# Exponentials of 1024 columns in place of 768 in a fused attention and expert kernel

## The chip, the core and the metric

The kernel runs on one core of a Trainium2 chip. The metric is the time on the device in microseconds (us), the median of several executions. The profile is one execution of the same program, and its span is a little shorter than the measured time. Engines: PE is the matrix engine, PEld its weight loads, DVE the vector engine, ACT the activation engine, POOL the general engine, and SP the engine whose instruction queue issues nearly all DMAs here.

## The reference

```python
# q, k, v: (4 batches, 8 heads, 768 positions, 64); proj: (64, 6)
q_bucket = sum over 6 bits of (q @ proj > 0) * 2**bit       # the same for k
mask     = q_bucket[..., :, None] == k_bucket[..., None, :]
scores   = where(mask, q @ k.T / 8, -1e9)
attn     = softmax(scores) @ v                               # (4, 8, 768, 64)
x        = attn, heads side by side                          # (3072, 512)
h        = x @ w_in                                          # (3072, 2048)
g        = h + sin(alpha * h)**2 / (alpha + 1e-9)
out      = g @ w_out                                         # (3072, 512)
```

## The kernel before

The program is a list of 16 pairs of heads, `pairs[i]`, four to a batch. A pair has 12 steps: two heads, six blocks of 128 keys each. A step multiplies one key block with all 768 queries (scores, transposed: keys in the partitions), takes the exponential on ACT, and some steps later "weighs" the values with it: six matmuls, one for each block of 128 queries. The hash mask is folded into the contraction as 12 extra rows, so a score matmul has 76 rows.

```python
HALF = S // 2                       # 384
banks = psum.tile([128, 8, 512], FP32, name="banks")
turns = deque(range(3))             # banks 0..5 are three slots of two banks

def slot(hold=False):
    n = turns.popleft()
    if not hold:
        turns.append(n)             # it comes round again at once; its readers are waited for
    return banks[:, 2 * n:2 * n + 2, :], n
def give_back(n):
    turns.append(n)

def attend(i, at_step, lag=3):
    ...
    for n in range(2 * SB):         # 12 steps
        hh, kb = divmod(n, SB)
        sc, _ = slot()
        for half in range(2):       # 384 queries in each bank
            nc.tensor.matmul(out=sc[:, half, 0:HALF], lhsT=ka[...key block kb...],
                             rhs=qa[0:KA, hh, half * HALF:(half + 1) * HALF], ...)
        e = e_pool.tile([128, S], BF16, name="e")
        nc.scalar.activation(out=e..., in_=sc[:, :, 0:HALF], func=AF.Exp, scale=SCALE)
        behind.append((i, hh, kb, e, accs[hh], xn))
        at_step(n)                  # the work between two steps, see below
        while len(behind) > lag + (i > NPAIR and behind[0][2] == 0):
            weigh(behind.pop(0))    # after key block 5: finish_head
```

`at_step(n)` puts parts of the preparation of later pairs, and a share of the contraction of the batch before (`g @ w_out`), between two steps. Pairs 1 to 5 are prepared on PE (hash matmuls, picking of bits, four times six transposes), and hold one of the three slots from their first transposes to the end of them; later pairs are prepared by DMA.

```python
def prepare_on_pe(i):
    ...                                   # hash and picking in bank 6 (i > 1)
    ps, held = slot(hold=True)            # at step 3 of pair i - 1
    for h in range(2):
        for t in (0, 1):
            ... six transposes into ps[0:KA, t, ...], copied out by DVE
            yield                         # steps 3, 4, 6, 7
    ...
    give_back(held)                       # at step 9

def prepare_by_dma(i):
    ...
    for a, nat in zip(aug, nats):         # step 6 of pair i - 2
        nc.sync.dma_start_transpose(out=a..., in_=nat...)               # qa<-qn, ka<-kn
    ps, held = slot(hold=True)            # step 10: hash matmuls, bits
    for a in range(4):
        nc.sync.dma_start(out=rows[...], in_=bits[a::4]...)             # rows<-bits
    ... give_back(held)                   # step 11
    ... copies of qa and ka               # step 1 of pair i - 1
    for t in range(2):                    # step 3 of pair i - 1
        for n in range(2):
            nc.sync.dma_start(out=aug[t][...], in_=rows...)             # qa<-rows, ka<-rows

def finish_head(i, hh, acc, xn):
    ...                                   # DVE: add the base, divide
    if hh == 1:
        nc.sync.dma_start_transpose(out=xt[b][:, hp, :]..., in_=xn...)  # xt<-xn
```

The expansion of a batch (`x @ w_in`, sine, square) reads `xt`; it comes after the first pair of the next batch, the last one at the end. So the program alternates: attention of five pairs, expansion, attention of four pairs, expansion, and so on.

The softmax here doesn't subtract the row's maximum and nothing guards it: scores larger than these inputs give would overflow.

Of the kernel before, what the change touches and what calls it, by code (L numbers as in the profile page):

```python
# [10 lines left out]
BF16 = mybir.dt.bfloat16  # L11
AF = mybir.ActivationFunctionType
# [11 lines left out]
def kernel(  # L24
# [11 lines left out]
    nc = tc.nc  # L36

    B, H, S, D = q.shape
# [3 lines left out]
    SB = S // 128  # L42
    NPAIR = H // 2
    NF = DFF // 128
    NP = DMODEL // 128
    HALF = S // 2
    KA = D + 2 * NB
    ON_PE = 6
    SCALE = 1.0 / (D ** 0.5)
# [5 lines left out]
    v32_pool = ctx.enter_context(tc.tile_pool(name="v32", bufs=3))  # L55
    v_pool = ctx.enter_context(tc.tile_pool(name="vp", bufs=4))
    w_pool = ctx.enter_context(tc.tile_pool(name="w32", bufs=3))
    e_pool = ctx.enter_context(tc.tile_pool(name="ep", bufs=6))
    x_pool = ctx.enter_context(tc.tile_pool(name="xp", bufs=3))
    xt_pool = ctx.enter_context(tc.tile_pool(name="xt", bufs=2))  # L60
    moe_pool = ctx.enter_context(tc.tile_pool(name="moe", bufs=3))
    g_pool = ctx.enter_context(tc.tile_pool(name="gp", bufs=1))
    o_pool = ctx.enter_context(tc.tile_pool(name="op", bufs=4))
    dram = ctx.enter_context(tc.tile_pool(name="scratch", bufs=4, space=bass.MemoryType.DRAM))
    psum = ctx.enter_context(tc.tile_pool(name="ps", bufs=1, space=bass.MemoryType.PSUM))

# [7 lines left out]
# [6 lines that stand above are left out]
# [102 lines left out]
    def turn_blocks(name, src):  # L182
        t = hash_pool.tile([128, 2, SB, 2, 32], FP32, name=f"{name}t")
        nc.vector.transpose(  # L184
            out=t.rearrange("p h s b c -> p (h s b c)"),
            in_=src.rearrange("p h s d -> p (h s d)"),
        )
        return t
# [32 lines left out]
    def prepare_on_pe(i):  # L221
# [3 lines left out]
        turned = [turn_blocks("q", q2)]  # L225
        nat = hash_pool.tile([128, SB, 4, KA], BF16, name="nat")
        for t, src in enumerate((q2, k2)):
# [22 lines left out]
        for s in range(SB):  # L250
# [5 lines left out]
        nc.vector.tensor_copy(  # L256
            out=nat[:, :, :, D:KA], in_=picked.rearrange("p s (j m) -> p s j m", j=4))
        yield
# [4 lines left out]
        for h in range(2):  # L263
            if (i, h) == (0, 1):
                ps = banks[:, 6:8, :]
            for t in ((1, 0) if i == 0 else (0, 1)):
                out = ps[0:KA, t, 0:HALF].bitcast(BF16)
                for s in range(SB):
                    nc.tensor.transpose(out[:, s * 128:(s + 1) * 128], nat[:, s, 2 * t + h], ident)  # L269
                if (i, h, t) == (0, 0, 1):  # L270
                    nc.scalar.copy(out=aug[t][0:KA, h, :], in_=out)
                else:
                    nc.vector.tensor_copy(out=aug[t][0:KA, h, :], in_=out)  # L273
                yield
# [64 lines left out]
    def finish_head(i, hh, acc, xn):  # L339
        b, hp = pairs[i]  # L340
        rden = hash_pool.tile([128, SB], FP32, name="rden")
        cols = acc[:, 0:SB * (D + 1)].rearrange("p (s e) -> p s e", e=D + 1)
        if len(operands[i]) > 4:
            total = x_pool.tile([128, SB, D + 1], FP32, name="total")
            nc.vector.tensor_tensor(  # L345
                out=total, in0=cols,
                in1=operands[i][4][:, hh].unsqueeze(1).to_broadcast([128, SB, D + 1]), op=ALU.add,
            )
            cols = total
        nc.vector.reciprocal(out=rden, in_=cols[:, :, D])  # L350
        nc.vector.tensor_tensor(  # L351
            out=xn[:, :, hh, :], in0=cols[:, :, 0:D],
            in1=rden.unsqueeze(2).to_broadcast([128, SB, D]), op=ALU.mult,
        )
        if hh == 1:
            nc.sync.dma_start_transpose(
                out=xt[b][:, hp, :].rearrange("p (s c) -> p s c", s=SB),
                in_=xn.rearrange("p s h d -> p (s h d)"),
            )

    behind = []

    def weigh(step):
        i, hh, kb, e, acc, xn = step
        vaug, vsum = operands[i][2:4]
        regions = acc[:, 0:SB * (D + 1)]

        apart = len(operands[i]) > 4
        if kb == 0 and not apart:
            nc.tensor.matmul(  # L370
                out=regions.rearrange("p (s e) -> p s e", e=D + 1),
                lhsT=empty,
                rhs=vsum[:, hh, :].unsqueeze(1).to_broadcast([128, SB, D + 1]),
                start=True, stop=False,
            )
        for qb in range(SB):
            nc.tensor.matmul(  # L377
                out=regions[:, qb * (D + 1):(qb + 1) * (D + 1)],
                lhsT=e[:, qb * 128:(qb + 1) * 128],
                rhs=vaug[:, hh, kb, :],  # L380
                start=(apart and kb == 0 and qb == 0), stop=(kb == SB - 1 and qb == SB - 1),
            )
        if kb == SB - 1:
            finish_head(i, hh, acc, xn)

    def attend(i, at_step, lag=3):
        b, hp = pairs[i]
        if b not in xt:
            xt[b] = xt_pool.tile([128, NPAIR, S], BF16, name="xt")
        qa, ka = operands[i][0:2]  # L390
        accs = [banks[:, 6, :], banks[:, 7 if i <= NPAIR else 6, :]]
        xn = x_pool.tile([128, SB, 2, D], BF16, name="xn")
        for n in range(2 * SB):
            hh, kb = divmod(n, SB)
            sc, _ = slot()
            for half in range(2):
                nc.tensor.matmul(  # L397
                    out=sc[:, half, 0:HALF],
                    lhsT=ka[0:KA, hh, kb * 128:(kb + 1) * 128],
                    rhs=qa[0:KA, hh, half * HALF:(half + 1) * HALF],  # L400
                    start=True, stop=True,
                )
            e = e_pool.tile([128, S], BF16, name="e")
            nc.scalar.activation(  # L404
                out=e.rearrange("p (h c) -> p h c", h=2), in_=sc[:, :, 0:HALF],
                func=AF.Exp, scale=SCALE,
            )
            behind.append((i, hh, kb, e, accs[hh], xn))
            at_step(n)

            while len(behind) > lag + (i > NPAIR and behind[0][2] == 0):
                weigh(behind.pop(0))
# [3 lines left out]
    def expand(b, at_chunk):  # L416
        g = g_pool.tile([128, NF, S], BF16, name="g")
        def close(F, s2, h):
# [3 lines left out]
                scalar=inv_alpha[:, F:F + 1],  # L422
                in1=h[:, :, 0:HALF],
                op0=ALU.mult, op1=ALU.add,
            )

        for F in range(NF):
            at_chunk(F, g)
            h = banks[:, 6:8, :] if F in (3, 7, 11) else slot()[0]
            for half in range(2):  # L430
                for p in range(NP):
                    nc.tensor.matmul(  # L432
                        out=h[:, half, 0:HALF],
                        lhsT=w_in_bf[:, p, F * 128:(F + 1) * 128],
                        rhs=xt[b][:, p, half * HALF:(half + 1) * HALF],
                        start=(p == 0), stop=(p == NP - 1),
                    )
            while behind:
                weigh(behind.pop(0))
            s = moe_pool.tile([128, S], BF16, name="s")  # L440
            nc.scalar.activation(  # L441
                out=s.rearrange("p (h c) -> p h c", h=2), in_=h[:, :, 0:HALF],
                func=AF.Sin, scale=alpha_sb[:, F:F + 1],
            )
            s2 = moe_pool.tile([128, S], BF16, name="s2")
            if F % 2 and (F < NF - 1 or b == B - 1):
                nc.scalar.activation(out=s2, in_=s, func=AF.Square)
            else:
                nc.vector.tensor_tensor(out=s2, in0=s, in1=s, op=ALU.mult)
            close(F, s2, h)  # L450
# [76 lines left out]
    with tc.manual_schedule():  # L527
# [43 lines left out]
        for i in range(n_pairs):  # L571
            b, hp = pairs[i]

            def at_step(n, i=i):
                for p in parts.get((i, n), ()):
                    if p not in under_way:
                        under_way[p] = prepare_on_pe(p) if p < ON_PE else prepare_by_dma(p)
                    next(under_way[p], None)
                if n == 6 and i + 4 < n_pairs:
                    load(i + 4)  # L580
                if n in (8, 11) and 0 < i <= NPAIR:
                    weigh_in(2)
                fill(1.9 if i > n_pairs - NPAIR else 1.75)

            attend(i, at_step)
            if hp == 0 and b > 0:
                drain()
                expand(b - 1, at_chunk)
                fill(8.0, 8)
        while behind:  # L590
            weigh(behind.pop(0))
# [32 lines left out]
```

## Time and profile before

| | before |
|---|---|
| time, median of 3 runs | 315.63 us |
| span of the profiled run | 311.2 us |
| exponentials | 192 of 768 columns, 811 ns each |
| PE / ACT / DVE busy | 97% / 76% / 65% |

One of the three runs took 347.28 us, over 10% more than the other two (313.70 and 315.63); it counts as slow. The profile, at full clock and with a span of 311.2 us, is not of that run.

The first lines are from the page of the kernel before: the busy times, then the groups of the exponentials and of the score matmuls. In a group, the first number is the busy time, the second the mean of one instruction, then the idle time of the engine ahead of it and what ended most of that.

```profile
PE 300.7 (97%) x3055; PEld 184.3 (59%) x3055; DVE 203.5 (65%) x348; ACT 237.8 (76%) x295; POOL 97.4 (31%) x180
...
L404 ACT ACTIVATE e<-banks 128x768 bf16<-128x768 f32 x192 | 147.6, 811 | 32.0 <-PE banks L397 24.2
...
L397 PE MATMUL banks<-qa,ka 76*128 76x384 bf16 x384 | 92.6, 325 | 1.4 <-DVE g L419 0.7
```

The Trainium skill ("Trainium Kernel Development and Optimization", section "Performance Expectations") calls matmul busy time a bad metric of how close a kernel is to its peak, because matmuls are pipelined, and in the timeline of PE below the six matmuls from 54.08 last until 54.43, while the next begin at 54.27.

How a step of the first stage runs is seen in the timeline of PE in the kernel before, here with a slot held (start, duration, engine, line, operation):

```profile
53.42 0.48 PE L397 MATMUL banks<-qa,ka 76*128 76x384 bf16 x2
53.75 0.50 PE L269 MATMUL banks<-ident,nat 128*76 128x128 bf16 x6
54.08 0.35 PE L377 MATMUL banks<-vaug,e 128*128 128x65 bf16 x6
54.27 0.49 PE L397 MATMUL banks<-qa,ka 76*128 76x384 bf16 x2
54.59 0.34 PE L377 MATMUL banks<-vaug,e 128*128 128x65 bf16 x6
```

And ACT in the timeline over the same stretch:

```profile
53.23 2.44 ACT L404 ACTIVATE e<-banks 128x768 bf16<-128x768 f32 x3
```

The two score matmuls of a step stand together. Transposes (L269) and weighing (L377) come after the slot is full, while ACT works on it, and ACT runs three exponentials without a gap over 0.1 us.

### The profile page before, as it was taken

The page shows a single profiled execution, that of the slowest core. Times are in us where ns is not written, and L with a number is a line of the kernel's source. Part 1 is how long each engine was busy: PE and PEld are TensorE (multiplying, and loading weights), DVE is VectorE, ACT ScalarE, POOL GpSimd, SP SyncE. Part 2 cuts the span into 40 slices and gives each one's busy share as a digit, 9 for nine tenths or more (in the row PEclk, how much of TensorE's full clock was granted, in tenths as well). Part 3 has the DMA queues.
Part 4 walks back from the last instruction along what each step waited for, and adds up shares of the span by engine and source line. Part 5 has one row for each costly group of instructions (what it writes and reads, how often), then busy time and mean ns, then how long its engine had stood idle before and what let it go on. Part 6 is the DMA issues. An engine that isn't in the chain of part 4 may idle for free.

```text
span 311.2 us, 7698 instructions
## 1 busy us (share of the span) xinstructions
PE 300.7 (97%) x3055; PEld 184.3 (59%) x3055; DVE 203.5 (65%) x348; ACT 237.8 (76%) x295; POOL 97.4 (31%) x180
## 2 busy tenths in 40 slices
PE   7899999999989999999999999999999999999996
PEld 6567767666555565666555565566555655565444
DVE  5587576799956656679955744669974424499411
ACT  1679989899887787789897787789897877599200
POOL 6748398426594433515000524410000000000000
PEclk9999999999999999999999999999999999999999
DMA  7935989999628588881027587860013311200021
GB/s 238 377 126 138 241 276 282 185 290 293 209 71 223 94 220 207 148 225 26 2 69 194 122 223 127 205 115 7 2 56 51 105 28 69 59 2 0 35 102 68
DMA packets 68724, 42.87 MB, mean 138 GB/s; under 512 B 46560, under 2 KB 63696, under 8 KB 68688
## 3 DMA queue, kind: packets, MB, share of 16 engines
q1 hardware_dynamic: 68576, 42.37, 52.5%
q8 instruction: 24, 0.39, 0.6%
q14 instruction: 12, 0.10, 0.1%
q10 hardware_dynamic: 112, 0.01, 0.0%
HBM read 28.01 MB, written 7.27 MB: 113 GB/s over the span
## 4 chain that ended last, share of the span: by engine, by line
PE 73%; DVE 9%; DMA 5%; ACT 5%; POOL 3%; issue 2%; SPq 1%; DVEq 0%; ACTq 0%; POOLq 0%
PE banks L432 24%; PE banks L467 22%; PE banks L397 13%; PE banks L377 8%; ACT e L404 5%; PE banks L193 3%; DMA v_3085<-in_v_dram 2%; DVE g L419 2%; PE banks L269 2%; DVE osb L475 1%; DMA k_148<-in_k_dram 1%; DMA ka<-kn 1%; DMA xt<-xn 1%; DVE qt L184 1%; DVE xn L351 1%
## 5 line engine op out<-in xcount | busy, mean ns | idle before, releaser
L404 ACT ACTIVATE e<-banks 128x768 bf16<-128x768 f32 x192 | 147.6, 811 | 32.0 <-PE banks L397 24.2
L467 PE MATMUL banks<-w_out_bf,g 128*128 128x512 bf16 (+1 forms) x400 | 103.8, 370 | 1.4 <-DVE osb L475 1.0
L397 PE MATMUL banks<-qa,ka 76*128 76x384 bf16 x384 | 92.6, 325 | 1.4 <-DVE g L419 0.7
L432 PE MATMUL banks<-xt,w_in_bf 128*128 128x384 bf16 x512 | 85.3, 326 | 0.4 <-DMA xt<-xn 0.2
L377 PEld LDWEIGHTS <-e 128*128 128x128 bf16 x1152 | 55.2, 97 | 27.4 <-issue 0.3
L432 PEld LDWEIGHTS <-w_in_bf 128*128 128x128 bf16 x512 | 49.7, 98 | 33.8 <-issue 1.2
L441 ACT ACTIVATE s<-banks,alpha_sb 128x768 bf16<-128x768 f32 x64 | 57.1, 893 | 11.5 <-PE banks L432 10.6
L377 PE MATMUL banks<-vaug,e 128*128 128x65 bf16 x1152 | 61.5, 193 | 0.0
L467 PEld LDWEIGHTS <-g 128*128 128x128 bf16 x400 | 38.5, 97 | 33.5 <-issue 3.1
L345 DVE TENSOR_TENSOR total<-banks,base 128x390 f32<-128x390 f32 x28 | 15.7, 561 | 39.8 <-PE banks L377 39.6
L475 DVE COPY osb<-banks 128x512 f32<-128x512 f32 (+1 forms) x25 | 16.7, 668 | 28.4 <-PE banks L467 28.4
L397 PEld LDWEIGHTS <-ka 76*128 76x128 bf16 x384 | 28.5, 98 | 10.7 <-issue 2.0
L210 POOL TENSOR_TENSOR vacc<-vacc,vaug 128x130 f32<-128x130 f32 x48 | 21.5, 448 | 3.8
L351 DVE TENSOR_TENSOR xn<-total,rden 128x384 bf16<-128x384 f32 x28 | 17.3, 618 | 1.0
L193 PE MATMUL banks<-qt,w_hash 128*32 128x192 f32 x128 | 13.6, 332 | 1.3 <-ACT e L404 0.5
L193 PE MATMUL banks<-kt,w_hash 128*32 128x192 f32 x128 | 13.5, 332 | 0.0
L269 PEld LDWEIGHTS <-nat 128*76 128x76 bf16 x144 | 10.4, 114 | 3.7 <-POOL nat L228 0.8
L269 PE MATMUL banks<-ident,nat 128*76 128x128 bf16 x144 | 11.5, 219 | 1.1 <-DVE nat L256 0.7
L273 DVE COPY qa<-banks 76x768 bf16<-76x768 bf16 x12 | 6.5, 546 | 5.7 <-PE banks L269 5.7
L193 PEld LDWEIGHTS banks<-qt,w_hash 128*32 128x32 f32 x128 | 5.9, 109 | 7.4 <-issue 2.5
L309 DVE TENSOR_SCALAR bits<-banks,side 128x192 bf16<-128x192 f32 x20 | 7.4, 412 | 3.2 <-ACT e L404 3.2
L203 POOL CAST vaug<-v_2876 128x768 bf16<-128x768 f32 x1 | 0.8, 829 | 25.4 <-PE banks L377 25.4
(275 smaller groups left out, 289.4 us busy)
## 6 DMA issues: line engine op xcount, KB each, us to landing
out_dram<-osb SPq DMA_DIRECT2D x23, 256.0 KB
rows<-bits SPq DMA_DIRECT2D x40, 24.0 KB
w_697<-in_moe_w_in_dram SPq DMA_DIRECT2D x1, 512.0 KB
w_738<-in_moe_w_in_dram SPq DMA_DIRECT2D x1, 512.0 KB
w_921<-in_moe_w_in_dram SPq DMA_DIRECT2D x1, 512.0 KB
w_964<-in_moe_w_in_dram SPq DMA_DIRECT2D x1, 512.0 KB
w_1145<-in_moe_w_in_dram SPq DMA_DIRECT2D x1, 512.0 KB
w_1186<-in_moe_w_in_dram SPq DMA_DIRECT2D x1, 512.0 KB
```

The costliest lines, as they stand in the source:

```text
L193: nc.tensor.matmul(out=ps[32 * j:32 * j + 32, 0:SB * 32].rearrange("p (s c) -> p s c", s=SB), lhsT=w_hash[:, blk].rearrange("p l a -> p (l ...
L210: nc.gpsimd.tensor_tensor(out=dst, in0=vacc[:, sb % 2], in1=vaug[:, :, sb], op=ALU.add)
L269: nc.tensor.transpose(out[:, s * 128:(s + 1) * 128], nat[:, s, 2 * t + h], ident)
L345: nc.vector.tensor_tensor(out=total, in0=cols, in1=operands[i][4][:, hh].unsqueeze(1).to_broadcast([128, SB, D + 1]), op=ALU.add,)
L351: nc.vector.tensor_tensor(out=xn[:, :, hh, :], in0=cols[:, :, 0:D], in1=rden.unsqueeze(2).to_broadcast([128, SB, D]), op=ALU.mult,)
L377: nc.tensor.matmul(out=regions[:, qb * (D + 1):(qb + 1) * (D + 1)], lhsT=e[:, qb * 128:(qb + 1) * 128], rhs=vaug[:, hh, kb, :], start=(apa ...
L397: nc.tensor.matmul(out=sc[:, half, 0:HALF], lhsT=ka[0:KA, hh, kb * 128:(kb + 1) * 128], rhs=qa[0:KA, hh, half * HALF:(half + 1) * HALF], s ...
L404: nc.scalar.activation(out=e.rearrange("p (h c) -> p h c", h=2), in_=sc[:, :, 0:HALF], func=AF.Exp, scale=SCALE,)
L432: nc.tensor.matmul(out=h[:, half, 0:HALF], lhsT=w_in_bf[:, p, F * 128:(F + 1) * 128], rhs=xt[b][:, p, half * HALF:(half + 1) * HALF], star ...
L441: nc.scalar.activation(out=s.rearrange("p (h c) -> p h c", h=2), in_=h[:, :, 0:HALF], func=AF.Sin, scale=alpha_sb[:, F:F + 1],)
L467: nc.tensor.matmul(out=o, lhsT=g[:, F, sub * 128:(sub + 1) * 128], rhs=w_out_bf[:, F, c0:c1], start=(F == 0), stop=(F == NF - 1),)
L475: nc.vector.tensor_copy(out=osb[:, c0:c1], in_=o)
```

## The change

The intent: a slot has two banks, 1024 columns, of which an exponential used 768. Four units of 256 queries now fill a slot whole, across the key blocks, so that three exponentials do the work of four and the fixed cost of an instruction is paid 144 times in place of 192. A step's 768 queries are three units, so four steps fill three slots. A score matmul cannot cross a bank: the Trainium skill ("PSUM — Partial Sum Buffer", section "The four PSUM rules") limits one matmul's output to one bank, 512 fp32 columns. Since the end of a step may now be in the next slot, weighing goes four steps behind in place of three (the `lag` of the code). Buffers for the wider `e` come out of one output buffer.

```diff
+    UNIT = S // 3
-    e_pool = ctx.enter_context(tc.tile_pool(name="ep", bufs=6))
+    e_pool = ctx.enter_context(tc.tile_pool(name="ep", bufs=5))
-    o_pool = ctx.enter_context(tc.tile_pool(name="op", bufs=4))
+    o_pool = ctx.enter_context(tc.tile_pool(name="op", bufs=3))
 ...
     def weigh(step):
 ...
         for qb in range(SB):
+            e, c = es[(3 * (hh * SB + kb) + qb // 2) // 4], (3 * (hh * SB + kb) + qb // 2) % 4
+            c = c * UNIT + qb % 2 * 128
             nc.tensor.matmul(
-                lhsT=e[:, qb * 128:(qb + 1) * 128],
+                lhsT=e[:, c:c + 128],
 ...
-    def attend(i, at_step, lag=3):
+    def attend(i, at_step, lag=4):
 ...
         for n in range(2 * SB):
             hh, kb = divmod(n, SB)
-            sc, _ = slot()
-            for half in range(2):
+            unit, end = 3 * n, 3 * n + 3
+            while unit < end:
+                if unit % 4 == 0:
+                    sc, _ = slot()
+                room = min(end, unit + 2 - unit % 2) - unit
+                u = unit % 4
                 nc.tensor.matmul(
-                    out=sc[:, half, 0:HALF],
+                    out=sc.rearrange("p b c -> p (b c)")[:, u * UNIT:(u + room) * UNIT],
                     lhsT=ka[0:KA, hh, kb * 128:(kb + 1) * 128],
-                    rhs=qa[0:KA, hh, half * HALF:(half + 1) * HALF],
+                    rhs=qa[0:KA, hh, (unit - 3 * n) * UNIT:(unit - 3 * n + room) * UNIT],
                     start=True, stop=True,
                 )
-            e = e_pool.tile([128, S], BF16, name="e")
-            nc.scalar.activation(... 768 columns ...)
-            behind.append((i, hh, kb, e, accs[hh], xn))
+                unit += room
+                if unit % 4 == 0:
+                    e = e_pool.tile([128, 4 * UNIT], BF16, name="e")
+                    nc.scalar.activation(
+                        out=e, in_=sc.rearrange("p b c -> p (b c)"), func=AF.Exp, scale=SCALE)
+                    es.append(e)
+            behind.append((i, hh, kb, es, accs[hh], xn))
             at_step(n)
```

More of the change, by code (lines that the diff above doesn't have):

```diff
@@ L363, in weigh @@
     def weigh(step):
-        i, hh, kb, e, acc, xn = step
+        i, hh, kb, es, acc, xn = step
         vaug, vsum = operands[i][2:4]
@@ L392, in attend @@
         xn = x_pool.tile([128, SB, 2, D], BF16, name="xn")
+        es, sc = [], None
         for n in range(2 * SB):
             hh, kb = divmod(n, SB)
-            sc, _ = slot()
-            for half in range(2):
+            unit, end = 3 * n, 3 * n + 3
[4 more added lines that the diff above has]
+                u = unit % 4
                 nc.tensor.matmul(
-                    out=sc[:, half, 0:HALF],
+                    out=sc.rearrange("p b c -> p (b c)")[:, u * UNIT:(u + room) * UNIT],
                     lhsT=ka[0:KA, hh, kb * 128:(kb + 1) * 128],
-                    rhs=qa[0:KA, hh, half * HALF:(half + 1) * HALF],
+                    rhs=qa[0:KA, hh, (unit - 3 * n) * UNIT:(unit - 3 * n + room) * UNIT],
                     start=True, stop=True,
                 )
-            e = e_pool.tile([128, S], BF16, name="e")
-            nc.scalar.activation(
-                out=e.rearrange("p (h c) -> p h c", h=2), in_=sc[:, :, 0:HALF],
-                func=AF.Exp, scale=SCALE,
-            )
-            behind.append((i, hh, kb, e, accs[hh], xn))
+                unit += room
[5 more added lines that the diff above has]
+            behind.append((i, hh, kb, es, accs[hh], xn))
             at_step(n)
```

## The prediction

> **What bounds it now.** The table of busy time has PE at 97% of the 311.2 us span, ACT 76%, DVE 65%. The chain of waits gives PE 73%, the exponentials 5%. By stretches of the timeline:
> - 10 to 61 us, first five head pairs (60 exponentials, no contraction to fill in): ACT and PE nearly balanced. From 43.7 to 59.4 us ACT runs 21 exponentials in 15.66 us, 0.74 us each, and the chain runs along them: ACT sets the pace.
> - Later attention stretches (132 exponentials): PE busy 12.0 of 12.0 us, ACT 9.2 to 9.8. In order of time one step is six weighing matmuls (0.18), two score matmuls (0.33) and about two contraction matmuls (0.43): 0.94 us. ACT waits for PE (24.2 us in the groups): PE sets the pace.
> - Expansion and the last 49 us hold no exponentials.
>
> **What changes.** 192 exponentials of 768 columns (811 ns each) become 144 of 1024. The Trainium skill, "ScalarE: Activation LUTs", section "What ACT_TABLE_LOAD costs", gives 186 ns + 0.833 ns a column, less 93 ns back to back; the trace roughly agrees (811 ns against 826). I estimate 1025 ns alone, 0.95 us back to back: 0.715 us a step against 0.74. Summed durations fall from 155.7 to 147.6 us. Score matmuls stay two a step (512 + 256 columns for 384 + 384, the same 0.33 us); weighing is the same, a step later.
>
> **On the critical path** is only the ACT-paced part, some 45 steps at 0.026 us: 1.2 us gained. PE-paced stages gain nothing; no PE work goes away.
>
> **Costs.**
> 1. An exponential now waits for four units written over two steps, so the PE work between steps lies inside the filling of a slot. While preparing by PE holds one of three slots (steps 3 to 9 of early pairs), ACT covers a refill with one exponential: 0.95 us against 0.69 us + the work between (0.16, or 0.46 with six transposes). ACT idles some 0.2 us twice a pair: 1.5 us in the first stage; plus 0.5 us at the start, where the first hash waits for a longer exponential.
> 2. Preparing by DMA takes a slot at step 10 for the hash. Before, its exponential had begun two steps earlier; now its last unit is written in step 9, and it ends about 1.4 us after step 9 begins, while PE reaches the hash after about 1.2. Estimate 0.2 us of PE idle, ten times: 2 us.
> 3. At each later attention start two slots take 2.67 steps, so PE stalls less for the last expansion slot: minus 0.5 us in all.
> 4. At the end one more step to weigh, and a longer last exponential: 0.3 us.
>
> Sum: -1.2 + 2.0 + 2.0 - 0.5 + 0.3 = about +2.5 us, under 1%.
>
> **Predicted: 317.5 us, 8 in 10 within 313.5 to 322. Faster by over 2%: 0.04; within 2%: 0.88; slower by over 2%: 0.08.**
>
> **What would show it.** 144 exponentials of about 1025 ns, their busy time about 8 us less, ACT idle up by as much. Later attention stretches: PE still 11.9 to 12.0 of 12 busy, lengths within 1%. The hash's wait for the exponential up from 2.3 us to about 4. First five pairs: same end within 1.5 us (61 us), with short ACT gaps in the unbroken row.
>
> **What would make it wrong.** If ACT were closer to the chain in later stages than its busy time says, it gains more. If coarser slots stall PE at every cycle and not only at the hash, or writing and reading the whole of both banks disturb each other, or one output buffer fewer makes the contraction wait for its store, it loses more, perhaps 6 to 8 us.

## More of the kernel before

`finish_head` of a batch's last pair falls into the first steps of the next pair.

A kernel in stages is read by stages. The next lines are the view of windows of the kernel before, cut at the first score matmul of each attention stage and at the first matmul of each expansion. Each has start:end, the length, busy time of each engine with its count of instructions, then the granted clock, the share of the DMA engines and GB/s. The last 45.28 us, the fourth expansion and contraction, are left out.

```profile
10.17:60.32 50.15, 47.60 (x809) 34.55 (x808) 36.41 (x72) 43.95 (x59) 35.56 (x65) 1.00 0.83 224
60.32:84.77 24.45, 24.26 (x164) 14.24 (x161) 21.89 (x29) 22.22 (x26) 10.40 (x10) 1.00 0.92 273
84.77:132.08 47.31, 46.48 (x520) 27.28 (x518) 28.84 (x57) 37.62 (x49) 24.05 (x46) 1.00 0.69 158
132.08:156.03 23.95, 23.95 (x164) 14.24 (x161) 21.51 (x28) 21.88 (x26) 5.96 (x10) 1.00 0.32 83
156.03:203.05 47.02, 46.44 (x519) 27.27 (x518) 27.05 (x55) 37.52 (x49) 13.86 (x27) 1.00 0.70 158
203.05:227.00 23.95, 23.95 (x165) 14.26 (x162) 21.50 (x28) 21.88 (x26) 0.63 (x1) 1.00 0.18 35
227.00:265.93 38.93, 38.23 (x390) 22.19 (x389) 16.21 (x33) 30.06 (x38) 0.00 (x0) 1.00 0.26 65
```

The first stage has no contraction in it, and there PE and ACT are close to each other (47.60 and 43.95 us of 50.15). In the later attention stages PE is nearly never idle and ACT is idle 9 to 10 us of each.

The timeline of the DMA queue of SP, around the end of the first pair of a batch:

```profile
122.08 2.53 SPq L315 DMA_DIRECT2D rows<-bits  x4
124.71 0.88 SPq L476 DMA_DIRECT2D out_dram<-osb  x1
125.69 1.50 SPq L356 DMA_TRANSPOSE xt<-xn  x1
128.62 0.63 SPq L329 DMA_DIRECT2D qa<-rows  x2
129.29 0.64 SPq L329 DMA_DIRECT2D ka<-rows  x2
```

The transposing store `xt<-xn` goes out before the queue stops to wait for `rows` to have landed (from 127.19 to 128.62).

## The result, and the profile after

| | before | after |
|---|---|---|
| time, median of 4 runs each | 314.66 us | 323.38 us |
| ratio of fast runs, 95% interval | | 1.0299 (1.0242 to 1.0357) |
| span of the profiled run | 311.2 us | 320.8 us |

Before has one more run here than in the earlier table, and the median has the slow run of 347.28 us in it; the ratio does not. Ratios throughout are the mean time of one kernel's fast runs over that of the other's of the same rounds, so not quite the ratio of the medians quoted. The change made the kernel 3% slower. Both profiled runs had the full clock.

The page after, the lines that answer to those of before:

```profile
PE 299.8 (93%) x3025; PEld 182.8 (57%) x3055; DVE 203.0 (63%) x348; ACT 234.3 (73%) x247; POOL 95.9 (30%) x180
...
L415 ACT ACTIVATE e<-banks 128x1024 bf16<-128x1024 f32 x144 | 144.1, 1022 | 41.5 <-PE banks L406 37.1
...
L406 PE MATMUL banks<-qa,ka 76*128 76x512 bf16 (+1 forms) x384 | 95.7, 325 | 5.1 <-ACT e L415 4.4
```

ACT has less to do, 144.1 us in place of 147.6, and waits more: 41.5 us in place of 32.0 ahead of exponentials. PE now waits for ACT ahead of score matmuls (4.4 us; 0.5 before), all of it in the first stage. Both engines wait for each other. (PE's 30 matmuls fewer are records missing from the trace, so its busy time is a little short.)

The windows after, cut at the same places:

```profile
9.99:65.72 55.73, 47.87 (x803) 33.35 (x801) 36.96 (x72) 43.22 (x44) 36.04 (x66) 1.00 0.68 202
65.72:90.97 25.25, 24.39 (x169) 14.43 (x167) 22.46 (x30) 22.44 (x26) 9.58 (x10) 1.00 0.94 267
90.97:138.24 47.27, 45.87 (x504) 27.03 (x512) 27.99 (x56) 36.56 (x37) 22.75 (x44) 1.00 0.59 150
138.24:163.59 25.35, 24.24 (x169) 14.44 (x167) 21.34 (x28) 21.91 (x26) 6.61 (x12) 1.00 0.38 93
163.59:211.27 47.68, 45.96 (x504) 27.03 (x512) 26.84 (x56) 36.59 (x37) 14.36 (x27) 1.00 0.65 152
211.27:236.73 25.46, 24.24 (x170) 14.43 (x168) 21.34 (x28) 21.90 (x26) 0.12 (x1) 1.00 0.22 41
236.73:275.28 38.55, 37.70 (x384) 22.13 (x389) 16.12 (x33) 29.04 (x29) 0.00 (x0) 1.00 0.26 66
```

Taking lengths line by line: the first stage grew by 5.58 us, the three expansions by 0.80, 1.40 and 1.51 (3.71 together), and the three later attention stages by -0.04, 0.66 and -0.38 (0.24 together). That is nearly all of the 9.6 us between the spans. The loss has two places, and neither is where most exponentials are.

**First place, the first stage.** The timeline of PE after, steps 4 to 7 of a pair, with a slot held:

```profile
57.48 0.49 PE L406 MATMUL banks<-qa,ka 76*128 76x512 bf16 x2
57.80 0.50 PE L270 MATMUL banks<-ident,nat 128*76 128x128 bf16 x6
58.14 0.34 PE L380 MATMUL banks<-vaug,e 128*128 128x65 bf16 x6
58.32 0.49 PE L406 MATMUL banks<-qa,ka 76*128 76x256 bf16 x2
58.65 0.35 PE L380 MATMUL banks<-vaug,e 128*128 128x65 bf16 x6
58.83 0.38 PE L406 MATMUL banks<-qa,ka 76*128 76x512 bf16 x1
59.77 0.27 PE L406 MATMUL banks<-qa,ka 76*128 76x256 bf16 x1 [0.55 <-ACT e L415]
59.87 0.50 PE L270 MATMUL banks<-ident,nat 128*76 128x128 bf16 x6
60.21 0.34 PE L380 MATMUL banks<-vaug,e 128*128 128x65 bf16 x6
60.39 0.49 PE L406 MATMUL banks<-qa,ka 76*128 76x256 bf16 x2
```

And the timeline of ACT after in the same stretch:

```profile
56.40 1.94 ACT L415 ACTIVATE e<-banks 128x1024 bf16<-128x1024 f32 x2
58.69 1.94 ACT L415 ACTIVATE e<-banks 128x1024 bf16<-128x1024 f32 x2 [0.35 <-PE banks L406]
60.98 1.02 ACT L415 ACTIVATE e<-banks 128x1024 bf16<-128x1024 f32 x1 [0.35 <-PE banks L406]
```

At 57.48 PE writes three units of a slot. The fourth follows at 58.32, behind six transposes and six weighing matmuls, and ACT sits idle for 0.35 us until 58.69. At 58.83 PE writes two of the three units of a step and has no slot for the third: one is held, one is being read, the one just filled waits. It idles 0.55 us until the exponential ends, writes one unit at 59.77, goes through transposes and weighing again, and writes the other three at 60.39. ACT has meanwhile nothing to read, 0.35 us again. The slot's filling is cut by the work between two steps, and with two slots to use, each engine waits for the other in turn. The loss is in all five pairs: from the first score matmul of one pair to that of the next, or to the expansion, they grew by 1.61, 1.09, 0.89, 0.72 and 1.29 us. ACT's gaps over 0.15 us ahead of exponentials went from 9 (5.1 us) to 18 (10.3 us) in this stage.

**Second place, the expansions.** The timeline of PE after, at the start of one:

```profile
138.24 0.65 PE L442 MATMUL banks<-xt,w_in_bf 128*128 128x384 bf16 x3
139.96 0.97 PE L442 MATMUL banks<-xt,w_in_bf 128*128 128x384 bf16 x5 [1.06 <-DMA xt<-xn]
```

PE waits 1.06 us for the transposing store of the batch's last pair. The DMA queue of SP after shows why it is late:

```profile
129.20 3.32 SPq L316 DMA_DIRECT2D rows<-bits  x4
132.62 0.56 SPq L486 DMA_DIRECT2D out_dram<-osb  x1
135.76 0.63 SPq L330 DMA_DIRECT2D qa<-rows  x2
136.44 0.64 SPq L330 DMA_DIRECT2D ka<-rows  x2
137.12 1.24 SPq L357 DMA_TRANSPOSE xt<-xn  x1
```

With weighing one step later, the head's end comes after the row transfers of step 3 in the program, and SP issues in order. The queue stands from 133.18 to 135.76 until `rows` has landed, and `xt<-xn`, which needs nothing of that, stands behind. Its own input, `xn`, was ready at 131.36 by the timeline of DVE. The Trainium skill ("DMA: Bandwidth & Descriptors", section "Two DMAs through the same engine are not ordered") says that the issuing engine must wait on the first DMA's semaphore before it issues a dependent one. This is that wait; here it took 2.6 us, and everything behind it on the issuing engine paid it.

### The profile page after: what moved, and what is told of

Same layout as the page of the kernel before. It is cut to its first block, busy times and chain, and to the rows that moved or that the text cites. A ratio compares the mean times of both kernels' runs of the same rounds, so it can differ in the third digit from the quotient of the medians.

```text
span 320.8 us, 7591 instructions
## 1 busy us (share of the span) xinstructions
PE 299.8 (93%) x3025; PEld 182.8 (57%) x3055; DVE 203.0 (63%) x348; ACT 234.3 (73%) x247; POOL 95.9 (30%) x180
## 4 chain that ended last, share of the span: by engine, by line
PE 77%; DVE 9%; DMA 5%; ACT 5%; issue 2%; SPq 1%; ACTq 0%; DVEq 0%
PE banks L442 24%; PE banks L477 22%; PE banks L406 15%; PE banks L380 10%; ACT e L415 4%; PE banks L194 3%; DMA xt<-xn 3%; PE banks L270 2%; DVE g L429 2%; DMA ka<-kn 1%; DMA k<-in_k_dram 1%; DVE osb L485 1%; DVE kt L185 1%; DVE s L459 1%; DVE qt L185 1%
## 5 line engine op out<-in xcount | busy, mean ns | idle before, releaser
L415 ACT ACTIVATE e<-banks 128x1024 bf16<-128x1024 f32 x144 | 144.1, 1022 | 41.5 <-PE banks L406 37.1
L477 PE MATMUL banks<-w_out_bf,g 128*128 128x512 bf16 (+1 forms) x370 | 98.4, 369 | 2.9 <-DVE osb L485 1.4
L406 PE MATMUL banks<-qa,ka 76*128 76x512 bf16 (+1 forms) x384 | 95.7, 325 | 5.1 <-ACT e L415 4.4
L429 DVE SCALAR_TENSOR_TENSOR g<-s,inv_alpha,banks 128x768 bf16<-128x768 bf16 x64 | 64.3, 1013 | 5.8 <-ACT s L457 2.0
L204 POOL CAST vaug<-v 128x768 bf16<-128x768 f32 x16 | 13.6, 851 | 73.0 <-PE banks L380 37.1
L457 ACT ACTIVATE s<-s 128x768 bf16<-128x768 bf16 x29 | 24.5, 843 | 0.9
L459 DVE TENSOR_TENSOR s<-s 128x768 bf16<-128x768 bf16 x35 | 20.8, 596 | 2.0 <-ACT s L451 2.0
L211 POOL TENSOR_TENSOR vacc<-vacc,vaug 128x130 f32<-128x130 f32 x48 | 20.3, 423 | 3.8
L185 DVE STREAM_TRANSPOSE qt<-q 128x768 f32<-128x768 f32 x16 | 15.5, 970 | 2.2 <-DMA q<-in_q_dram 2.1
L185 DVE STREAM_TRANSPOSE kt<-k 128x768 f32<-128x768 f32 x16 | 15.1, 945 | 0.2 <-DMA k<-in_k_dram 0.2
```

The costliest lines, as they stand in the source:

```text
L185: nc.vector.transpose(out=t.rearrange("p h s b c -> p (h s b c)"), in_=src.rearrange("p h s d -> p (h s d)"),)
L211: nc.gpsimd.tensor_tensor(out=dst, in0=vacc[:, sb % 2], in1=vaug[:, :, sb], op=ALU.add)
L406: nc.tensor.matmul(out=sc.rearrange("p b c -> p (b c)")[:, u * UNIT:(u + room) * UNIT], lhsT=ka[0:KA, hh, kb * 128:(kb + 1) * 128], rhs=qa ...
L415: nc.scalar.activation(out=e, in_=sc.rearrange("p b c -> p (b c)"), func=AF.Exp, scale=SCALE)
L429: nc.vector.scalar_tensor_tensor(out=g[:, F, :].rearrange("p (h c) -> p h c", h=2), in0=s2.rearrange("p (h c) -> p h c", h=2), scalar=inv_ ...
L457: nc.scalar.activation(out=s2, in_=s, func=AF.Square)
```

## The experiments

The theory: the loss is two losses. (1) In the first stage, the work between two steps lies inside the filling of a slot while one of three slots is held. (2) Weighing four steps behind puts the transposing store behind the row transfers. Rivals: the lag alone; 1024 columns as such; the cut filling whether or not a slot is held. "First stage" is always measured as in the windows above, from the first score matmul to the first expansion matmul.

| run | kernel, and what was done to it | ratio to before (95%) | first stage, us | expansions 1 to 3, us |
|---|---|---|---|---|
| - | before | 1 | 50.15 | 24.45, 23.95, 23.95 |
| - | after | 1.0299 (1.0242 to 1.0357) | 55.73 | 25.25, 25.35, 25.46 |
| e1_lag3 | after, lag three | 1.0291 (1.0236 to 1.0345) | 56.07 | 24.59, 23.94, 23.94 |
| e2_whole | after, slots filled in one go | 1.0148 (1.0098 to 1.0199) | 50.70 | 25.10, 24.99, 25.19 |
| e3_rows4 | after, row transfers a step later | 1.0242 (1.0176 to 1.0307) | slow run | 24.13, 24.13, 24.13 |
| e4_before_cut | before, filling cut (wrong result) | 1.0301 (1.025 to 1.0352) | 57.35 | 25.03, 23.95, 23.95 |
| e5_before_cut2 | before, filling cut, mended | 1.0352 (1.0309 to 1.0395) | 59.73 (clock 0.94) | 25.03, 23.95, 23.94 |
| e6_whole_rows4 | after, both mendings | 0.9997 (0.9958 to 1.0037) | 51.08 | 24.13, 24.12, 24.13 |
| e7_after_nohold | after, no slot held | 1.0248 (1.0192 to 1.0304) | 54.34 | 24.59, 25.08, 24.94 |
| e8_before_nohold | before, no slot held | 1.0074 (1.0039 to 1.0109) | 54.28 | 24.71, 23.94, 23.95 |
| e9_after_nohold2 | as e7, transposes two steps apart | 1.0204 (1.0161 to 1.0246) | 52.01 | 24.76, 26.32, 25.12 |
| e10_before_nohold2 | as e8, transposes two steps apart | 1.0029 (0.9974 to 1.0084) | 50.97 | 24.40, 24.12, 23.95 |
| e11_before_lag4 | before, lag four | 1.0123 (1.0079 to 1.0167) | 50.67 | 24.74, 25.06, 25.00 |
| e12_best | after, whole, rows, no slot held | 1.0054 (1.0019 to 1.0089) | 51.37 | 24.61, 24.18, 24.13 |

e1 to e8 ran on one chip in two sessions (before there: median 313.75 us for e1 to e4, 314.45 for e5 to e8), e9 to e12 on another (313.37). One run each of e3 and e10 was slow and is not in the ratio.

### e1_lag3: the lag put back

```diff
-    def attend(i, at_step, lag=4):
+    def attend(i, at_step, lag=3):
```

> The changed kernel with weighing three steps behind again, the rest as changed. Theory (two separate losses: 5.6 us in the first attention stage because the work between two steps lies inside the filling of a slot, and about 3 us in the expansions because the later weighing puts the transposing store of the last pair behind the row transfers in the one DMA queue): the three expansions after an attention stage lose their waits for that transpose and come back by 2.5 to 3.5 us in all (from 25.3, 25.4, 25.5 us to about 24.4, 24.0, 24.0), the first stage stays at 55 to 56.5 us; ratio to before 1.018 to 1.024. Rival A (the lag alone makes the loss): ratio below 1.008 and the first stage back near 50 us. Rival B (the lag has nothing to do with it): ratio stays at 1.03.

Median 323.14 us. The stages behave as the theory says: the expansions fell back to 24.59, 23.94 and 23.94 us, 3.6 us together, and the first stage stayed at 56.07. The time did not follow: the expected ratio was missed, and the measured one is that of rival B, although its reason (the lag does nothing) does not hold. The three later attention stages took 49.52, 48.36 and 39.43 us, 3.8 us more than after. Of the first of them about 1 us is a wait of the contraction for the copy of its weights, which POOL makes (PE waited 1.1 us for it in all; nothing in the list of waits of the changed kernel); another part is the hash waiting for exponentials (3.3 us of PE's waits, 1.5 after). The rest was not followed. So undoing the lag alone is worth nothing in this kernel, although it takes away what it was said to take away: other waits stood ready behind.

### e2_whole: all of a slot in one go

```diff
-            unit, end = 3 * n, 3 * n + 3
+            end = (3 * n + 3 + 3) // 4 * 4        # to the end of the slot; unit starts at 0
             while unit < end:
+                m = unit // 3                      # the step that the unit belongs to
 ...             # lhsT and rhs by m in place of n
```

A step that opens a slot also writes its last units, ahead of their own step. There are as many matmuls and exponentials as in the changed kernel.

> The changed kernel, four steps behind, but each slot is filled by consecutive matmuls: a step that opens a slot writes all four units of it, the last of them ahead of its own step, so no transposes, hashing or weighing lie inside a filling; same matmuls, same 144 exponentials. Theory: the first attention stage falls from 55.7 us to 50 to 52 us, ACT's gaps of 0.35 us vanish, and the expansions keep their loss; ratio to before 1.007 to 1.015. Rival (coarser slots as such: a slot of 1024 columns with only two slots free starves ACT however it is filled, or reading and writing whole banks disturb each other): the first stage stays above 54 us, ratio 1.025 to 1.03.

Median 318.39 us, inside what was expected, but not all of ACT's gaps vanished: five of 0.34 to 0.39 us are left in the last four pairs of the first stage. The line of the first stage, in the view of windows of this run:

```profile
10.23:60.93 50.70, 46.15 (x803) 33.79 (x801) 36.24 (x70) 43.46 (x46) 36.13 (x66) 1.00 0.75 216
```

It is 5.03 us shorter than after (55.73), with 1024 columns and lag four unchanged. The expansions kept their loss, 25.0 to 25.2 us. Wide exponentials, and reading and writing two whole banks, are not what costs the first stage; the interruption of the filling is.

### e3_rows4: the row transfers one step later

```diff
-            at = [(i - 2, n) for n in (3, 6, 10, 11)] + [(i - 1, n) for n in (1, 3)]
+            at = [(i - 2, n) for n in (3, 6, 10, 11)] + [(i - 1, n) for n in (1, 4)]
```

> The changed kernel, four steps behind, but the row transfers of the pairs prepared by DMA are issued one step later (step 4 for step 3), so that the transposing store of a batch's last pair comes ahead of them in the DMA queue again. Theory: the waits of the expansion's first matmuls for that transpose (2.5 us in the profile) fall to under 0.5 us although the lag is still four, the first stage keeps its 55.7 us; ratio to before 1.020 to 1.026. Rival (the lag itself delays the expansion, by the weighing left over and by the later end of a head): the expansions stay at 25.3 us or more, ratio stays at 1.03.

Median 322.76 us, the ratio as expected, though its interval makes the run itself unclear at 2%. The profiled execution was a slow one (clock 0.973 on the mean; 0.94 in the two stretches that were slow), so its first stage says nothing. In the three expansions the clock was 1.00, and each took 24.13 us with PE busy 24.13, here the second in the view of windows of this run:

```profile
147.25:171.38 24.13, 24.13 (x170) 14.44 (x167) 21.34 (x28) 21.91 (x26) 6.96 (x12) 1.00 0.35 90
```

No wait for the transpose is left in them, at lag four. Of the three expansions' 3.71 us this is 3.67 (the sum of 25.25, 25.35 and 25.46 less three times 24.13). Lag as such costs them next to nothing; the order in the DMA queue does.

### e4_before_cut and e5_before_cut2: the filling cut in the kernel before

```diff
-            sc, _ = slot()
-            for half in range(2):
+            for step, half in ([(n, 0)] if n == 0 else []) + [(n, 1), (n + 1, 0)]:
+                if step == 2 * SB:
+                    continue
+                if half == 0:
+                    nxt, _ = slot()
                 ... the same matmul, for this step and half
+                if half == 1: ...the exponential of nxt...     # mended: here; e4 had it behind the loop
```

> The kernel before, with 192 exponentials of 768 columns, three steps behind, but the first half of the next step's scores is written before the work between two steps and the second half after it, so the filling of every slot is cut by that work. Nothing else is changed. Theory: the cut filling alone slows the first attention stage, from 50.2 us to 53 to 57 us, with short gaps of ACT that wait for score matmuls, and leaves the later attention stages within 1 us each; ratio to before 1.008 to 1.022. Rival (the loss needs 1024-column slots): first stage within 1 us of 50.2, ratio 0.997 to 1.004.

> The cut filling in the kernel before once more, mended: the run before this gave a wrong result because an exponential stood behind the opening of a slot in the program, and once, in the first pair, that slot was its own. Now the exponential stands ahead of it. Theory as before: the first attention stage goes from 50.2 to 54 to 58 us with 768-column exponentials and nothing else changed; ratio 1.02 to 1.035. Rival (the loss needs 1024-column slots, and the wrong run was slow through its fault): first stage under 52 us, ratio under 1.01.

e4 gave a wrong result (relative error 0.075): in the first pair, after a slot had been given back and another held, the next slot to come up was one whose exponential was not in the program yet. Its median was 323.14 us, ratio 1.0301, more than the 1.008 to 1.022 expected. e5 mends that, is correct, and took 325.59 us, ratio 1.0352, at the upper edge of what was expected; its first stage, 59.73 us, is above it, but the clock in that window was 0.94. In e4 it was 57.35 us at full clock, just above the 53 to 57 expected. With 768-column exponentials and lag three, cutting the filling slows the first stage by 7 us or more, so the cut suffices by itself. The edit is a little harsher than the change: it also takes the next slot half a step early, always.

### e6_whole_rows4: both mendings

> Both mendings in the changed kernel at once: slots filled by consecutive matmuls, and the row transfers issued one step later; still 144 exponentials of 1024 columns, four steps behind. Theory (two separate losses that add): first stage about 50.7 us as with the first mending, the expansions 24.1 us each as with the second; sum against the kernel with the first mending alone about 2.9 us less, ratio to before 1.003 to 1.010. If the losses hide one another, or the gain is given back to another wait, ratio stays at 1.012 or more. If 1024 columns are worth anything by themselves, ratio under 1.000.

The edit is e2 and e3 together. Median 314.71 us against 314.45 of before. Windows of this run, the first stage and the first expansion:

```profile
10.48:61.56 51.08, 46.13 (x802) 33.86 (x801) 36.80 (x71) 43.40 (x46) 35.18 (x65) 1.00 0.73 215
61.56:85.69 24.13, 24.13 (x170) 14.44 (x167) 21.68 (x31) 21.04 (x25) 8.71 (x9) 1.00 0.91 276
```

Both losses are gone, and the time is that of the kernel before: the interval of the ratio, 0.9958 to 1.0037, holds 1. It is a little better than the 1.003 to 1.010 expected. The expansions account for 2.9 us against e2 (75.28 to 72.38 us) and the attention stage between the second and third for another 1.5 (48.00 to 46.53). In e2 that stage had one wait of 1.63 us of the contraction for DVE's copy of its output; DVE stood before it, for 3.6 us, waiting for the transposed `qa`, which stood in the same queue behind the same row transfers. In e6 the contraction waits 0.5 us in that stage in place of 2.0. So in this place the queue's order cost through DVE too.

### e7 to e10: no slot held

```diff
 def prepare_on_pe(i):                  # for i > 1
-            ps = banks[:, 6, :]
+            ps = banks[:, 7, :]
 ...
-        ps, held = slot(hold=True)     # now only for i <= 1
-                out = ps[0:KA, t, 0:HALF].bitcast(BF16)
+                out = ps[0:KA, 0:HALF].bitcast(BF16)       # i > 1: bank 7 for all four
 ...
-        accs = [banks[:, 6, :], banks[:, 7 if i <= NPAIR else 6, :]]
+        accs = [banks[:, 6, :], banks[:, 6, :]]
-            while len(behind) > lag + (i > NPAIR and behind[0][2] == 0):
+            while len(behind) > lag + (behind[0][2] == 0):
 # e9 and e10 as well:
-                (i - 1, n) for n in (1, 3, 4, 6, 7, 7, 9, 11)]
+                (i - 1, n) for n in (1, 3, 5, 7, 9, 9, 10, 11)]
```

> The changed kernel with its cut filling, four steps behind and its row transfers late, but preparing by PE (pairs 2 to 5) uses the one bank 7 and takes no slot, so that the exponentials keep three slots; both heads of a pair gather in bank 6. Theory: with a third slot the cut filling no longer starves ACT, for two exponentials cover a filling in place of one; first stage from 55.7 to 50 to 53 us, ratio to before 1.013 to 1.022. Rival (the cut alone matters, three slots or two): the first stage stays above 54.5 us, ratio 1.026 or more.

> The same freeing of the slot in the kernel before: pairs 2 to 5 prepared in bank 7, both heads of a pair in bank 6, nothing else. Theory: the exponentials of the first stage run closer to their own 0.69 us (some of those before took 0.84 us where transposes lie between), so the first stage gains 0.5 to 2.5 us; ratio 0.992 to 0.999. Rival (the slot matters only where the filling is cut): first stage unchanged within 0.5 us, ratio 0.998 to 1.004.

To free bank 7 for the transposes, both heads of a pair gather their sums in bank 6. Both expectations were missed. e7 took 322.93 us, its first stage 54.34; e8 took 316.97 us, its first stage 54.28, 4 us longer than before. With one bank for all transposes, PE waits for the copy that empties it: it idles 3.2 us ahead of transposes in the first stage of e7 and 3.1 in that of e8 (0.9 after, 0.4 before), of which the profile puts 1.5 and 2.6 us down to that copy. The two first stages agree within 0.1 us, which is what the theory wants (with three slots the cut filling costs nothing), but both are slowed by the new wait, so this pair alone shows little. The next pair of runs takes more than half of this idle time away (1.4 and 1.0 us are left).

> The changed kernel without a held slot as in the run before, but its transposes into the single bank 7 now lie two steps apart (steps 3, 5, 7, 9), because in the run before PE waited 5.3 us ahead of transposes for the copy that empties that bank. The cut filling, the lag of four and the late row transfers stay. Theory (the cut filling starves ACT only because one slot is held): PE's gaps ahead of score matmuls stay near 2 us (8.8 in the changed kernel), those ahead of transposes fall under 2 us, and the first stage is within 1 us of the same arrangement in the kernel before (next run); I expect 50.5 to 53 us. Rival (the cut starves ACT with three slots too): first stage 3 us or more above the next run's.

> The same arrangement in the kernel before: no slot held by pairs 2 to 5, transposes two steps apart in bank 7. Theory: exponentials run at 0.69 to 0.74 us more often, first stage 49 to 52 us (54.3 us in the run before with transposes one step apart), the rest as before; ratio 0.994 to 1.004. It is the partner of the run before it: if the cut filling costs nothing with three slots, the two first stages agree within 1 us.

(The expectation of e9 quotes 5.3 us for the wait ahead of transposes in e7 and 8.8 us for PE's gaps ahead of score matmuls in the changed kernel. In the traces PE idled 3.2 and 5.0 us there, counted in the first stage.) e9 took 319.91 us and e10 314.55 us. PE's gaps ahead of score matmuls are 1.2 us in e9. The windows of their first stages, e9 and then e10:

```profile
10.06:62.07 52.01, 46.73 (x803) 33.06 (x802) 35.48 (x71) 42.52 (x45) 36.59 (x67) 1.00 0.77 210
```

```profile
10.03:61.00 50.97, 46.80 (x809) 33.06 (x807) 35.81 (x72) 43.52 (x60) 35.66 (x65) 1.00 0.80 219
```

With a slot held, the change costs the first stage 5.58 us; with none held, 1.04 us (52.01 less 50.97), and the filling is cut in both. So the held slot is a part of the cause: it takes both. The difference is at the edge of the 1 us that was written down. The first stage of e10 is not better than before's 50.15, so the hope of a gain for the kernel before fell.

### e11_before_lag4: the lag alone, in the kernel before

```diff
-    def attend(i, at_step, lag=3):
+    def attend(i, at_step, lag=4):
```

> The kernel before with one part of the change alone: weighing four steps behind. Theory (lag four puts the transposing store behind the row transfers): the first stage stays within 1 us of 50.2, the expansions grow from 24.4, 24.0, 23.9 us to about 25.2, 25.3, 25.4, with PE waiting about 1 us in each for the transpose; ratio 1.006 to 1.012. Rival (the later weighing only hurts together with 1024 columns): expansions unchanged, ratio under 1.004.

Median 317.65 us, ratio 1.0123, just past the upper end of what was expected. The first stage hardly moves (50.67), and the DMA queue of SP in this run has the order of the changed kernel:

```profile
130.68 0.63 SPq L329 DMA_DIRECT2D qa<-rows  x2
131.35 0.64 SPq L329 DMA_DIRECT2D ka<-rows  x2
132.03 1.25 SPq L356 DMA_TRANSPOSE xt<-xn  x1
```

The expansions grew by 0.29, 1.11 and 1.05 us, less than after. A further 1.6 us is in the later attention stages (47.93, 48.47 and 38.44 us against 47.31, 47.02 and 38.93), where the contraction waited 3.2 us for DVE's output copies (1.0 before) and 1.0 us for POOL's copy of its weights, and DVE 7.2 us for the transposed `qa` (4.1 before). With no wide exponential anywhere, the lag alone costs about 1.2% (interval 0.8 to 1.7%).

### e12_best: everything that helps, at once

> The arrangement meant to keep what wide exponentials can give: 144 of 1024 columns, slots filled by consecutive matmuls, row transfers one step later, no slot held in the first stage, transposes two steps apart. Theory: wide exponentials save at most 0.012 us a step (0.904 us for 1024 columns back to back against 0.690 for 768), so 0.7 us in the first stage at best; first stage 49 to 51.5 us, expansions 24.1 us, ratio 0.990 to 1.002. If ACT set the pace of the first stage by itself, ratio under 0.990.

The edits of e2, e3 and e9 together. Median 315.12 us, ratio 1.0054 (1.0019 to 1.0089), above what was expected, and not better than e6, whose interval overlaps this one. The bank that takes the place of the slot brings its own waits: in the first stage PE waits 1.5 us for DVE ahead of matmuls into bank 6 and 0.8 us for the copies out of bank 7; in e6 the like comes to 0.3 us. No version with wide exponentials was faster than the kernel before.

## Why the prediction was wrong

The prediction named 317.5 us, within 2%; measured were 323.38 us and 3% slower.

- **"only the ACT-paced part, some 45 steps at 0.026 us: 1.2 us gained".** The size was too large, and no run shows even the sign in the time. Back to back, the smallest distance from one exponential's start to the next is 0.690 us in the trace before and 0.904 us in the traces with 1024 columns. That is 0.690 and 0.678 us a step, a gain of 0.012 us and not 0.026, or 0.7 us over the 60 steps of the first stage. ACT's busy time fell by as much (43.95 us before, 43.22 after), but the stage itself was never shorter: with both losses mended, in e6, it took 51.08 us against 50.15. The 0.74 us that I read as ACT's pace was 0.05 us more than the smallest distance; I take that for short waits, which was argued and not followed.
- **"Costs, 1": the filling cut by the work between steps.** The mechanism was right. e2 (filling in one go: 5.0 us of the 5.6 back), e4 and e5 (cutting it in the kernel before: 7 us or more lost) and e9 with e10 (no slot held: 1.0 us in place of 5.6) show it. The term was mis-sized: 2.0 us predicted, or 0.8 with the gain taken off, and 5.58 us measured. The prediction let ACT idle 0.2 us twice a pair. The timeline shows 0.35 us at two successive refills, since one from 59.77 to 60.98 took 1.21 us against an estimate of 1.15, while the exponential that covered it took 0.92 in place of 0.95. And it left out that PE stands too, 0.55 us, because it finds no slot in the middle of a step and can do none of the work behind; these waits of PE for exponentials came to 4.4 us, 0.5 before.
- **"weighing is the same, a step later".** This is the step that failed outright. It was counted as free but for 0.3 us at the end. The same matmuls one step later changed the order of a DMA queue, and the three expansions grew by 3.7 us. e3 takes that loss away at lag four by moving the row transfers only; e11 brings loss into the kernel before by the lag only, 1.2%. The new order could be seen before any run, in the order of SP's instructions in the two programs; the prediction did not look at SP.
- **"Costs, 2": the hash waiting for a later exponential.** The wait is there and larger than said: the weight loads and matmuls of the hash waited 8.5 us for exponentials, 2.3 before, where about 4 was predicted. But the three later attention stages together grew by only 0.24 us, not by 2. Most of it is the wait of weight loads (7.0 us), which start ahead of their matmuls (those of six transposes at 48.14, the first of the matmuls at 48.25).
- **"Costs, 3"**, minus 0.5 us at the starts of later attention stages, was not measured by itself. The stages' sum of 0.24 us leaves room for it.
- **"Costs, 4"**, 0.3 us at the end: the part after the last attention stage grew by 0.21 us (45.28 to 45.49). Right.
- **"One output buffer fewer makes the contraction wait"** was named as a risk. It was not tested by itself. e6 has the fewer buffers and runs as fast as before. Of the other risks it named, "coarser slots stall PE" came true in the first stage only (the 4.4 us), and that reading and writing whole banks disturb each other is not seen in e2.

By place, the prediction's sum against the profile: the first stage +0.8 us said and 5.58 measured, the expansions 0 and 3.71, the later attention stages 1.5 and 0.24, the end 0.3 and 0.21.

The two losses do not simply add. Mending the queue's order is worth 1.5% once slots are filled in one go (e2 to e6), and about 0.6% without that (after to e3, intervals that overlap); putting the lag back is worth nothing in the changed kernel (e1). What stays open is where all of e1's attention stages' 3.8 us went.

## What to carry to other kernels

A wider instruction saves only the fixed cost that is not hidden already, so measure its distance back to back at the width you have; here about 50 ns of it were left to save, once in four exponentials. When the unit of a hand-over grows past the unit of the loop, check what now lies between its first and last write, and do it with the fewest buffers the loop ever has: fill it in one go, or keep a buffer free. When a lag or an order in the program moves, compare the issue order of every engine, the DMA queue too: an instruction that waits for a DMA holds all that stand behind it (2.6 us here).

## What the Trainium skill lacked or had wrong

- "ScalarE: Activation LUTs", section "What ACT_TABLE_LOAD costs": 186 ns + 0.833 ns a column, less 93 ns back to back, gives 826 and 1039 ns alone and 733 and 946 back to back, for 768 and 1024 columns. The runs show 811 and 1022 ns alone, and 690 and 904 ns back to back. The slope agrees (214 ns for 256 columns, 0.836 ns each); the fixed part back to back is about 50 ns (690 less 768 times 0.833 is 50, 904 less 1024 times 0.833 is 51), about half of the 93 that this section leaves. The exponentials here read PSUM, which the section does not tell apart. "Perfetto Trace Analysis", section "Optimizing Scalar/DVE Operations", does: it gives ScalarE about 93 ns an instruction on SBUF and about 51 ns on PSUM, and the second is what the runs show. The prediction worked from the first section, which made wide instructions look twice as worthwhile as they were.
- "DMA: Bandwidth & Descriptors": the page tells to wait on the issuing engine before a dependent DMA, and that such waits take place on its sequencer, but does not draw the consequence that unrelated DMAs behind it on that engine are held back. Here it was 2.6 us once, and 3.7 us over three expansions.
- "Perfetto Trace Analysis", section "Optimization Strategy", takes gaps that repeat on the engine that should be saturated as a possible sign of too few buffers; it has nothing on two engines that starve each other through a buffer. The sign here was idle time on both sides, each ended by the other: ACT 37.1 us waiting for score matmuls (24.2 before) and PE 4.4 us for exponentials (0.5 before).
